# A list scheduler's time model in a one-core attention and mixer kernel: holding and seeing as two figures, block means on GpSimd, one weight sum later

## The chip, the cores and the metric

The kernel runs on one core of a Trainium2 chip. The core has five engines that run their own instruction streams and wait for one another by semaphores: TensorE (PE in the profile, its weight loads PEld), VectorE (DVE), ScalarE (ACT), GpSimd (POOL) and SyncE (SP), which here only issues DMA transfers. The metric is the device time of one execution in microseconds. A profiled execution gives, for each instruction, its engine, start and length, from which the views quoted below are made.

## The reference

Four batches of attention with eight heads of width 64 over 768 positions, each followed by a mixer with two pairs of matrices. All of it is float32.

```python
def _attn_ref(q, k, v):
    block, window = (32, 16)
    k_sum = k.reshape(B, H, nb, block, D).max(axis=3)
    v_sum = v.reshape(B, H, nb, block, D).mean(axis=3)
    scores_l = scale * np.matmul(q, k.transpose(0, 1, 3, 2))
    mask_l = np.abs(pos[:, None] - pos[None, :]) < window
    scores_s = scale * np.einsum('bhsd,bhnd->bhsn', q, k_sum) + np.log(block)
    scores_l_m = np.where(mask_l, scores_l, -1000000000.0)
    a = softmax(np.concatenate([scores_l_m, scores_s], axis=-1))
    return np.matmul(a, np.concatenate([v, v_sum], axis=2))

def _moe_ref(x, w_tok1, w_tok2, w_ch1, w_ch2):
    xt = x.transpose(0, 2, 1)
    h = np.maximum(xt @ w_tok1, 0.0) @ w_tok2
    u = x + h.transpose(0, 2, 1)
    h2 = np.maximum(u @ w_ch1, 0.0) @ w_ch2
    return u + h2
```

A position sees the keys less than 16 away from it and 24 block keys, each the maximum of 32 keys; the values of the block keys are the means of 32 values. The token matrices are 768 x 256 and 256 x 768, the channel matrices 512 x 1536 and 1536 x 512.

## The kernel before

**Attention.** Heads go in pairs, four pairs a batch; `p` counts the pairs over all batches, `g` is the half of the 768 positions. For a pair and a half, `scores` (products on PE, L467, line 467 of the kernel) multiplies queries with 96 window keys and 24 block keys. Then DVE adds the mask and takes each row's minimum (L481), and ACT takes the exponential and its row sums (L491). `turn` transposes the result on PE (L529) and copies it out with ACT (L540). In the last two batches the transposes go by DVE and DRAM instead. `weighted` multiplies with the values (L599) and scales the result with the reciprocal sums (L605 on POOL, L625 and L610 on DVE). `key_blocks` makes the block keys on DVE (L335, L344). For batch 0 alone `first_means` makes the block values: PE sums the values into two halves (L361), ACT copies one half (L372), DVE adds the other half, and the result, 24 rows for each head, is spread over twelve places of the value tile. For a pair's first head DVE adds once (`once`, L382) and POOL copies to all places (`spread`, L387); for its second head DVE adds straight into all places (`both`, L375).

**Mixer.** `tok1` (L753, L800, L837) and `tok2` (L912, L920) apply the token matrices, `ch1` (L981) and `ch2` (L1024) the channel matrices; float32 products are made from a high and a low part of each operand, three products each. Batches 0 to 2 run the channel matrices in slots: 12 slots of 512 columns and 12 of 256, in each of which stand one `ch1`, one `ch2` and a share of the next batch's attention. Batch 3, `last_batch` (L1251), uses sums and differences of weight blocks. These are made ahead by `mixes` (L1095 to L1152): POOL adds high and low parts and combines blocks, ACT and POOL split the result, and it is stored to DRAM. The table `MIXES` says in which slot each starts.

**Weights.** They arrive as 64-bit words and are decoded by `w_tick`, 30 ticks of two loads each: ACT takes an absolute value (`absolute`, L1665), POOL limits it (`clamp`, L1669), DVE does three steps (`shift` L1674, `sign` L1681, `low` L1688); from tick 3 on ACT and POOL split the result in high and low parts (L1712, L1718). Ticks 0 to 2 hold the first token matrix, 3 to 5 the second, and from 6 on two ticks belong to each of the twelve blocks of the channel matrices. All tick loads use buffers in which attention's tiles stood or will stand.

**Order.** The program does not emit instructions at once. `add` notes each piece of work with its engine, a duration in microseconds, what it reads and writes, a rank, and works that it may not start before (`behind`). `Plan._order` then simulates the engines: at each moment every free engine takes its ready work of the lowest rank, and of those the oldest. The order of the starts found so is the order in which the instructions are emitted; on the chip each engine keeps it and waits by semaphores. So a duration in `add` changes no instruction, but can change each engine's order. The ranks are `R_H, R_EVAC, R_ATT, R_LATER, R_W = range(5)` and `R_MIX = 6`; loads and stores have rank 0. The weight steps of ticks below `TOKT` have `R_ATT`, the later ones `R_W`.

In the simulation a work holds its engine for its duration; a DMA of `kb` thousand bytes starts when the earlier ones are through, at `RATE` per microsecond, and is seen `LAND` later. A work on another engine may start `LATE[engine]` after the end:

```python
late = self.LATE[e] if n.eng != e else 0.0
at = w.end + late if whole else now
```

Of the kernel before, what the change touches and what calls it, by code (L numbers as in the profile page):

```python
# [14 lines left out]
AF = mybir.ActivationFunctionType  # L15
# [63 lines left out]
class Plan:  # L79
    LATE = {"pe": 0.3, "act": 0.15, "dve": 0.15, "pool": 0.2, "sp": 0.0}  # L80
    RATE, LAND = 250.0, 2.2
# [46 lines left out]
    def _order(self):  # L128
# [9 lines left out]
        idle = {e: 0.0 for e in self.LATE}  # L138
        queues = {e: [] for e in self.LATE}
# [5 lines left out]
        for w in self.works:  # L145
            if not left[w]:
                release(w)
        while events:
# [5 lines left out]
            for e, queue in queues.items():  # L154
# [45 lines left out]
def tile_attention_mixer(  # L200
# [89 lines left out]
    def load(slot, view, src, kb, reads=(), behind=()):  # L290
        return add(
            "sp", 0.06, lambda: nc.sync.dma_start(out=view(slot.t), in_=src),
# [13 lines left out]
    def load_v(n):  # L306
# [7 lines left out]
        state["v"] = load(slot, lambda t: t[:WIN], vw[b, h], 295)  # L314
        if b > 0:
            s = vs[b]
            add(
                "sp", 0.06,
# [9 lines left out]
    def key_blocks(p):  # L328

        if p >= B * NP:  # L330
# [3 lines left out]
            "dve", 0.98,  # L334
# [8 lines left out]
            "dve", 0.33,  # L343
# [7 lines left out]
    def first_means(p):  # L351
# [22 lines left out]
        def both(n):  # L374
            nc.vector.tensor_tensor(  # L375
                out=v_t[n].t[WIN:NC],
                in0=half(1, 1).unsqueeze(1).broadcast_to([NB, NT, D]),
                in1=s.t[WIN:NC, D:].unsqueeze(1).broadcast_to([NB, NT, D]), op=ALU.add,
            )

        def once():
            nc.vector.tensor_tensor(  # L382
                out=s.t[WIN:NC, :D], in0=half(0, 1), in1=s.t[WIN:NC, :D], op=ALU.add
            )

        def spread(n):
            nc.gpsimd.tensor_copy(  # L387
                v_t[n].t[WIN:NC], s.t[WIN:NC, :D].unsqueeze(1).broadcast_to([NB, NT, D])
# [3 lines left out]
            "pe", 0.9, sums, reads=[(v_t[2 * p], 0), (v_t[2 * p + 1], 0)], writes=[(pt, 0)],  # L392
            rank=R_H,
        )
        for j in range(2):
# [3 lines left out]
        add("dve", 0.2, once, reads=[(pt, 0)], writes=[(s, 0)], rank=R_EVAC)  # L399
        add(  # L400
            "pool", 0.95, lambda: spread(2 * p), reads=[(s, 0)], writes=[(v_t[2 * p], 1)],
            rank=R_ATT,
        )
        add(
            "dve", 0.95, lambda: both(2 * p + 1), reads=[(pt, 0), (s, 1)],
            writes=[(v_t[2 * p + 1], 1)], rank=R_EVAC,
# [1490 lines left out]
```

## Time and profile before

| | |
|---|---|
| median of 3 runs | 560.07 us (559.93 to 560.61) |
| profiled execution | 559.61 us |
| its span, first to last instruction | 557.8 us |
| instructions | 12595 |
| TensorE's granted clock, mean | 1.000 |
| DMA, mean | 181 GB/s, 101.10 MB |

The profiled execution is one of its own, so sums over its rows are made against 559.61 us. The span ends 1.8 us below it. The profile's views that are read below: the busy time of each engine over the whole span, the same for stretches of the span, the waits of an engine (for which instruction, how long in all, how often, and the longest), groups of instructions by line with minimum, median and maximum of their lengths, and instructions in order of time, where several alike in a row are merged (`x24`) and the time in brackets is the engine's idle time just before and who ended it. The columns of a stretch are: from and to, length, busy time of PE, PEld, DVE, ACT and POOL with their counts, TensorE's clock, the DMA engines' busy share, and GB/s.

### The profile page before, as it was taken

The numbers are of one execution on the slowest core, as the hardware profiler recorded it, in microseconds if no ns is written. First come the engines' busy times: TensorE is split into PE (matmuls) and PEld (weight loads), VectorE is DVE, ScalarE is ACT, GpSimd is POOL, SyncE is SP. The second block draws the span as 40 slices with busy tenths as digits, with TensorE's granted clock in tenths as the row PEclk, the third lists the DMA queues.
The fourth block names the chain that finished last, engine by engine and source line by source line (L and its number), as shares of the span: only waits on it lengthen the run. The fifth ranks groups of instructions, "written<-read, shape, count | busy, mean of one in ns | idle before, by whom it ended". The sixth has DMA issues, their size and how long they took to land.

```text
span 557.8 us, 12595 instructions
## 1 busy us (share of the span) xinstructions
PE 544.0 (98%) x4557; PEld 479.6 (86%) x4557; DVE 330.3 (59%) x922; ACT 251.9 (45%) x784; POOL 246.8 (44%) x362
## 2 busy tenths in 40 slices
PE   7699999999999999999999999999999999999997
PEld 4588788888999978888799988878889999999997
DVE  4788999979365355454543247454352065669992
ACT  4786666625585344332323325343433453356410
POOL 0326687835574932310067404378769963000000
PEclk9999999999999999999999999999999999999999
DMA  8963668755668138768595316787696543932742
GB/s 277 330 189 108 215 209 249 240 163 190 203 187 251 42 131 226 198 207 226 146 253 137 104 29 196 160 237 198 171 259 168 135 155 116 333 95 81 219 134 85
DMA packets 125743, 101.10 MB, mean 181 GB/s; under 512 B 70000, under 2 KB 105456, under 8 KB 125680
## 3 DMA queue, kind: packets, MB, share of 16 engines
q1 hardware_dynamic: 125680, 100.29, 60.7%
q8 instruction: 36, 0.59, 0.5%
q14 instruction: 27, 0.22, 0.1%
HBM read 70.18 MB, written 28.31 MB: 177 GB/s over the span
## 4 chain that ended last, share of the span: by engine, by line
PE 90%; ACT 4%; DVE 3%; POOL 2%; issue 1%; ACTq 0%
PE acc L1024 27%; PE hp L981 27%; PE sc L467 4%; PE av L599 4%; PE up L920 3%; PE t1q L837 3%; ACT e L491 2%; PE x L1251 2%; PE y L1251 2%; PE z L1251 2%; PE pz L1251 2%; PE t1q L800 2%; PE up L1213 2%; PE warm L1731 1%; PE pw L1251 1%; PE pv L1251 1%
## 5 line engine op out<-in xcount | busy, mean ns | idle before, releaser
L1024 PE MATMUL acc<-h,w2h 128*128 128x256 f32 (+1 forms) x576 | 153.8, 339 | 0.0
L981 PE MATMUL hp<-u,w1h 128*128 128x256 f32 (+1 forms) x576 | 143.8, 339 | 0.0
L1024 PEld LDWEIGHTS acc<-h,w2h 128*128 128x128 f32 x576 | 100.6, 188 | 13.8 <-ACT h L993 1.6
L981 PEld LDWEIGHTS hp<-u,w1h 128*128 128x128 f32 x576 | 98.0, 189 | 12.4 <-issue 1.1
L981 PE MATMUL hp<-u,w1l 128*128 128x256 f32 (+1 forms) x288 | 96.9, 336 | 0.0
L491 ACT ACTIVATE e<-e,den 128x120 f32<-128x120 f32 x192 | 73.3, 384 | 52.0 <-DVE den L481 39.1
L1024 PE MATMUL acc<-h,w2l 128*128 128x256 f32 (+1 forms) x288 | 96.4, 335 | 0.0
L998 DVE SCALAR_TENSOR_TENSOR h<-hp,h 128x512 fp32r<-128x512 f32 (+1 forms) x72 | 39.9, 554 | 90.9 <-ACT h L993 90.7
L993 ACT ACTIVATE h<-hp 128x512 fp32r<-128x512 f32 (+1 forms) x72 | 35.2, 489 | 114.7 <-PE hp L981 114.5
L981 PEld LDWEIGHTS hp<-u,w1l 128*128 128x128 f32 x288 | 54.4, 189 | 5.8
L1024 PEld LDWEIGHTS acc<-h,w2l 128*128 128x128 f32 x288 | 54.2, 188 | 5.2
L481 DVE CUSTOM_DVE_ANT_0 e<-sc,mask_sb 128x120 f32<-128x120 f32 x192 | 41.7, 277 | 16.8 <-PE sc L467 16.2
L605 POOL TENSOR_SCALAR rec<-den 128x6 f32<-128x6 f32 x32 | 8.6, 269 | 66.1 <-ACT e L491 64.0
L491 ACT ACTIVATION_READ_ACCUMULATOR e<-e,den 128x1 f32 x192 | 36.1, 188 | 0.0
L1064 POOL TENSOR_TENSOR ot<-ot,u 128x512 f32<-128x512 f32 (+1 forms) x24 | 24.4, 1042 | 19.7 <-DVE ot L1056 18.2
L467 PE MATMUL sc<-k,q 64*64 64x120 f32 x768 | 28.0, 271 | 3.7 <-DVE den L481 2.2
L467 PEld LDWEIGHTS sc<-k,q 64*64 64x64 f32 x768 | 20.5, 132 | 12.5 <-issue 6.2
L920 PE MATMUL up<-wt2h,t 128*128 128x512 f32 (+1 forms) x96 | 28.4, 354 | 0.6 <-DVE t L739 0.6
L599 PEld LDWEIGHTS av<-v,eT 120*64 120x64 f32 x768 | 24.0, 138 | 4.7 <-issue 2.8
L599 PE MATMUL av<-v,eT 120*64 120x64 f32 x768 | 26.5, 224 | 0.9 <-PE hp L981 0.4
L335 DVE TENSOR_REDUCE ks<-k 128x24 f32<-128x768 f32 x16 | 15.2, 948 | 20.5 <-DMA k<-in_kw 20.5
L423 DVE TENSOR_REDUCE vs<-vb 96x8 f32<-96x256 f32 (+1 forms) x40 | 17.8, 458 | 9.4 <-DMA vb<-in_vb 9.3
(248 smaller groups left out, 1042.7 us busy)
## 6 DMA issues: line engine op xcount, KB each, us to landing
w<-in_w_ch SPq DMA_DIRECT2D x48, 256.0 KB
k<-in_kw SPq DMA_DIRECT2D x16, 720.0 KB
v<-in_vw SPq DMA_DIRECT2D x32, 288.0 KB
q<-in_q SPq DMA_DIRECT2D x16, 384.0 KB
away<-e SPq DMA_DIRECT2D x16, 384.0 KB
eT<-away SPq DMA_DIRECT2D x64, 96.0 KB
w<-in_w_tok SPq DMA_DIRECT2D x12, 256.0 KB
vb<-in_vb SPq DMA_DIRECT2D x32, 96.0 KB
```

The lines of the kernel that those rows point to most:

```text
L423: lambda: nc.vector.tensor_reduce(out=s.t[:VB, rows], in_=slot.t[:VB], axis=AX, op=ALU.add),
L467: nc.tensor.matmul(tiles[j].t[c * QT : (c + 1) * QT, i * NC : (i + 1) * NC], lhsT=qt.t[rows, t * QT : (t + 1) * QT], rhs=kt.t[rows, t, :], ...
L481: nc.vector.tensor_tensor_reduce(out=e.t[:, j, i * P : i * P + NC], in0=tiles[j].t[:, i * NC : (i + 1) * NC], in1=mask_sb[:, mv, :], op0=A ...
L491: nc.scalar.activation(ei, ei, AF.Exp, bias=den_t[n].t[:, 1, T : T + 1], scale=-1.0, accum_out=den_t[n].t[:, 0, T : T + 1],)
L599: nc.tensor.matmul(pv[cs, T], lhsT=eT[:NC, T % (TT // 2), cs], rhs=v.t[:NC, 2 * T + c], start=True, stop=True,)
L920: nc.tensor.matmul(pt.t[:, :nt], lhsT=t1.t[:, part, ks], rhs=w.t[:, k, h0 : h0 + nt], start=(far and k == 0 and i == 0), stop=(k == DTOK / ...
L981: nc.tensor.matmul(pt.t[:, :nt], lhsT=block(w, f, c), rhs=us[c].t[:, part], start=(i == 0), stop=(i == len(ops) - 1),)
L993: lambda: nc.scalar.activation(h.t[:, 0], pt.t[:, :nt], AF.Relu),
L998: lambda: nc.vector.scalar_tensor_tensor(out=h.t[:, 1], in0=pt.t[:, :nt], scalar=0.0, in1=h.t[:, 0].bitcast(F32), op0=ALU.max, op1=ALU.sub ...
L1024: nc.tensor.matmul(slot.t[:, c0 : c0 + nt], lhsT=block(w, f, o), rhs=h.t[:, part], start=(f == 0 and w == "w2h" and part == 0 and o % n == 0),
L1064: lambda view=view, u=u: nc.gpsimd.tensor_tensor(out=view(), in0=view(), in1=u.t[:, 1].bitcast(F32), op=ALU.add),
L1251: nc.tensor.matmul(pt.t[:, :cols], lhsT=w[wp][0](), rhs=z.t[:, zp], start=first and seen == 0, stop=final and seen == 3 * len(ops) - 1, sk ...
```

## The change

The planner gets two figures for each work in place of one: how long it holds its engine (`took`) and when its result is seen (`took` and `DRAIN` of its engine, and `NOTICE` of the engine that waits). Engines begin at `FIRST` and not at 0; a work that must only start behind another is seen `SEEN` later; a DMA begins `BEGIN` after its issue, at a higher `RATE` and with a shorter `LAND`. Some 60 durations are set anew; a DMA issue is now 0.44 on SP where most had 0.06, and some `kb` are raised. `first_means` loses `both`: for each head DVE adds once and POOL spreads, and both heads' copies have rank `R_ATT`. `TOKT` goes from 3 to 7. The weight sum `('w2', 4)` of batch 2 goes from slot 14 to slot 21, and such late sums are put behind their slot's `ch1`.

```diff
 class Plan:
-    LATE = {"pe": 0.3, "act": 0.15, "dve": 0.15, "pool": 0.2, "sp": 0.0}
-    RATE, LAND = 250.0, 2.2
+    FIRST = {"pe": 1.17, "act": 1.9, "dve": 0.85, "pool": 1.2, "sp": 0.7}
+    DRAIN = {"pe": 0.16, "act": 0.1, "dve": 0.08, "pool": 0.045, "sp": 0.0}
+    NOTICE = {"pe": 0.035, "act": 0.035, "dve": 0.035, "pool": 0.09, "sp": 0.035}
+    SEEN, BEGIN, LAND, RATE = 0.06, 1.34, 1.0, 375.0
...
-        idle = {e: 0.0 for e in self.LATE}
+        idle = dict(self.FIRST)
...
+        for e, at in idle.items():
+            heapq.heappush(events, (at, -1, None))
...
-                    dma = max(dma, now) + w.kb / self.RATE
+                    dma = max(dma, now + self.BEGIN) + w.kb / self.RATE
                     w.end = dma + self.LAND
                 else:
-                    w.end = now + w.took
+                    w.end = now + w.took + self.DRAIN[e]
...
-                    late = self.LATE[e] if n.eng != e else 0.0
-                    at = w.end + late if whole else now
+                    if not whole:
+                        at = now + self.SEEN
+                    elif n.eng != e:
+                        at = w.end + self.NOTICE[n.eng]
+                    else:
+                        at = idle[e] if e == "pe" else w.end
...
-        def both(n):
+        def once(j):
+            cs = slice(j * D, (j + 1) * D)
             nc.vector.tensor_tensor(
-                out=v_t[n].t[WIN:NC],
-                in0=half(1, 1).unsqueeze(1).broadcast_to([NB, NT, D]),
-                in1=s.t[WIN:NC, D:].unsqueeze(1).broadcast_to([NB, NT, D]), op=ALU.add,
-            )
...
+                out=s.t[WIN:NC, cs], in0=half(j, 1), in1=s.t[WIN:NC, cs], op=ALU.add
+            )
...
+        def spread(j):
             nc.gpsimd.tensor_copy(
-                v_t[n].t[WIN:NC], s.t[WIN:NC, :D].unsqueeze(1).broadcast_to([NB, NT, D])
-            )
...
+                v_t[2 * p + j].t[WIN:NC],
+                s.t[WIN:NC, j * D : (j + 1) * D].unsqueeze(1).broadcast_to([NB, NT, D]),
+            )
...
-        add("dve", 0.2, once, reads=[(pt, 0)], writes=[(s, 0)], rank=R_EVAC)
...
+        for j in range(2):
+            add(
+                "dve", 0.2, lambda j=j: once(j), reads=[(pt, 0)], writes=[(s, j)], rank=R_EVAC
+            )
+            add(
+                "pool", 0.95, lambda j=j: spread(j), reads=[(s, j)],
+                writes=[(v_t[2 * p + j], 1)], rank=R_ATT,
+            )
...
         add(
-            "pe", 0.95, products, reads=[(qt, 0), (kt, 0), (kt, 1)],
+            "pe", 0.776, products, reads=[(qt, 0), (kt, 0), (kt, 1)],
             writes=[(t, 0) for t in tiles], rank=R_H, behind=behind,
...
             add(
-                "pe", 0.5, flip, reads=[(e, (j, i)) for i in range(TT // 2)], writes=[(pt, 0)],
+                "pe", 0.33, flip, reads=[(e, (j, i)) for i in range(TT // 2)], writes=[(pt, 0)],
...
-    def mixes(k, i, tag, half=None):
+    def mixes(k, i, tag, half=None, behind=()):
...
-    TOKT = 3
+    TOKT = 7
...
-        stt = 0.7 if room else 0.85
+        stt = 0.6 if room else 0.75
...
-        add("dve", 0.69, shift, reads=parts, writes=[bkey], rank=rank)
+        add("dve", 0.596, shift, reads=parts, writes=[bkey], rank=rank)
...
-    add("pe", 7.0, warm_up, reads=[(warm, 0)], writes=[(pw, 0)])
+    add("pe", 4.6, warm_up, reads=[(warm, 0)], writes=[(pw, 0)])
...
-    MIXES = {..., (2, 14): [('w2', 4, 'h')], ...}
+    MIXES = {..., (2, 21): [('w2', 4, 'h')], ...}
...
-                mixes(*job)
+                mixes(*job, behind=here if slot > 14 else ())
```

More of the change, by code (lines that the diff above doesn't have):

```diff
@@ L137, in _order @@
         ready = {w: 0.0 for w in self.works}
-        idle = {e: 0.0 for e in self.LATE}
-        queues = {e: [] for e in self.LATE}
+        idle = dict(self.FIRST)
+        queues = {e: [] for e in idle}
         events, done, dma = [], [], 0.0
@@ L291, in load @@
         return add(
-            "sp", 0.06, lambda: nc.sync.dma_start(out=view(slot.t), in_=src),
+            "sp", 0.44, lambda: nc.sync.dma_start(out=view(slot.t), in_=src),
             reads=reads, writes=[(slot, 0)], kb=kb, behind=[*behind, *state["gate"]],
@@ L620, in weighted @@
             add(
-                "pool", 0.15, whole, reads=[(den, ("sum", T)) for T in range(TT)],
+                "pool", 0.166, whole, reads=[(den, ("sum", T)) for T in range(TT)],
                 writes=[(rec, 0)], rank=R_H,
@@ L628, in weighted @@
             add(
-                "dve", 0.57, scaled, reads=[(pt, 0), (rec, 0)], writes=[(x2, (hp % 2, j))],
+                "dve", 0.465, scaled, reads=[(pt, 0), (rec, 0)], writes=[(x2, (hp % 2, j))],
                 rank=R_EVAC,
@@ L737, in split_t1 @@
         add(
-            "dve", took + 0.05,
+            "dve", took + 0.065,
             lambda: nc.vector.scalar_tensor_tensor(
@@ L759, in tok1 @@
         add(
-            "pe", 2.8, products, reads=x_keys(b, p) + [(wt1, i) for i in range(3)],
+            "pe", 2.68, products, reads=x_keys(b, p) + [(wt1, i) for i in range(3)],
             writes=[(pt, 0)], rank=R_ATT,
@@ L808, in tok1x @@
             add(
-                "pe", 1.45, products, reads=[(s, i) for s in parts for i in range(2)],
+                "pe", 1.44, products, reads=[(s, i) for s in parts for i in range(2)],
                 writes=[(pt, 0)], rank=R_ATT,
@@ L843, in tok1_all @@
             add(
-                "pe", 1.37, products, reads=[(s, i) for s in (xs, ws) for i in range(2)],
+                "pe", 1.376, products, reads=[(s, i) for s in (xs, ws) for i in range(2)],
                 writes=[(pt, 0) for pt in pts], rank=R_ATT,
@@ L926, in tok2 @@
         add(
-            "pe", spent(nt, 0.75, 1.45) if far else spent(nt, 1.1, 2.0), products,
+            "pe", spent(nt, 0.707, 1.4) if far else spent(nt, 0.93, 1.837), products,
             reads=([] if far else x_keys(b, p)) + t1_keys(b, p) + T2_KEYS,
@@ L946, in tok2 @@
             )
-            eng, took = (("dve", spent(nt, 0.42, 0.62)), ("pool", spent(nt, 0.7, 1.2)))[half]
+            eng, took = (("dve", spent(nt, 0.34, 0.623)), ("pool", spent(nt, 0.7, 1.25)))[half]
             add(
@@ L1034, in ch2 @@
                 add(
-                    "pe", 3 * n * nt / 2220, lambda i=i: products(range(n * i, n * i + n)),
+                    "pe", 3 * n * nt / 2190, lambda i=i: products(range(n * i, n * i + n)),
                     reads=reads, writes=[(slot, 0)], rank=R_W,
@@ L1039, in ch2 @@
             add(
-                "pe", 12 * nt / 2220, lambda: products(range(NC4)), reads=reads,
+                "pe", 12 * nt / 2170, lambda: products(range(NC4)), reads=reads,
                 writes=[(slot, 0) for slot in slots], rank=R_W,
@@ L1098, in mixes @@
             add(
-                "pool", n * 0.0043 + 0.19, lambda x=x, f=f: whole(x, f),
-                reads=weight_keys(names, f), writes=[(a, x)], rank=R_MIX,
+                "pool", n * 0.0043 + 0.145, lambda x=x, f=f: whole(x, f),
+                reads=weight_keys(names, f), writes=[(a, x)], rank=R_MIX, behind=behind,
             )
@@ L1219, in tok2_last @@
         add(
-            "pe", 1.08, products, reads=t1_keys(b, p) + T2_KEYS, writes=[(pt, 0)], rank=R_ATT
+            "pe", 1.05, products, reads=t1_keys(b, p) + T2_KEYS, writes=[(pt, 0)], rank=R_ATT
         )
         add(
-            "dve", 0.56,
+            "dve", 0.474,
             lambda: nc.vector.tensor_tensor(
@@ L1259, in product @@
         return add(
-            "pe", 3 * len(ops) * cols / 2190, run, reads=list(reads), writes=[(pt, 0)], rank=R_W
+            "pe", 3 * len(ops) * cols / 2215, run, reads=list(reads), writes=[(pt, 0)], rank=R_W
         )
@@ L1736, in tile_attention_mixer @@
     add(
-        "sp", 0.06, lambda: nc.sync.dma_start(out=mask_sb, in_=mask), writes=[("mask", 0)], kb=184
+        "sp", 0.44, lambda: nc.sync.dma_start(out=mask_sb, in_=mask), writes=[("mask", 0)], kb=184
     )
```

135 lines of the change are left out of this document (62 added, 73 removed).

## The prediction

> **What bounds the kernel now.** I read the page's first part, then stretches of the span side by side, then TensorE's waits before 64 us. In the page:
> ```profile
> PE 544.0 (98%) x4557; PEld 479.6 (86%) x4557; DVE 330.3 (59%) x922; ACT 251.9 (45%) x784; POOL 246.8 (44%) x362
> ```
> TensorE (PE) is busy 544.0 of 557.8 us, so a change that leaves every matmul in place can win back at most the 13.8 us between. The view by stretches says where they lie (PE, then PEld, DVE, ACT, POOL; each busy time is followed by its count):
> ```profile
> 0.00:8.00 8.00, 6.83 (x45) 2.98 (x49) 1.92 (x5) 1.28 (x1) 0.76 (x7) 1.00 0.75 270
> 8.00:20.00 12.00, 8.61 (x230) 6.53 (x222) 8.98 (x53) 10.57 (x50) 1.30 (x3) 1.00 1.04 326
> 20.00:32.00 12.00, 7.85 (x119) 6.25 (x109) 10.49 (x36) 7.35 (x25) 4.18 (x6) 1.00 1.00 295
> 32.00:44.00 12.00, 12.00 (x288) 10.93 (x284) 10.59 (x43) 10.75 (x41) 5.14 (x9) 1.00 0.52 149
> 44.00:56.00 12.00, 11.70 (x116) 10.06 (x116) 9.53 (x28) 8.02 (x27) 7.80 (x11) 1.00 0.34 107
> 56.00:64.00 8.00, 7.17 (x54) 6.21 (x54) 7.22 (x14) 5.66 (x15) 5.13 (x8) 1.00 0.70 221
> 64.00:554.00 490.00, 489.60 (x3746) 436.64 (x3744) 281.03 (x750) 208.30 (x628) 222.50 (x321) 1.00 0.60 176
> 554.00:558.00 4.00, 0.27 (x2) 0.00 (x0) 0.56 (x1) 0.00 (x0) 0.00 (x0) 0.92 0.13 49
> ```
> From 64 to 554 us PE idles 0.40 us, at clock 1.00. The last 3.7 us are the last sum and its store, which the change leaves alone. The rest is at the front: 3.39 us from 8 to 20, 4.15 from 20 to 32, 1.13 from 44 to 64. There another engine is full: ACT 10.57 of 12 us in the first, DVE 10.49 of 12 in the second. The DMA share is full from 8 to 32 us as well, but no DMA stands among PE's waits up to 64 us:
> ```profile
> PE t1p L753 <- DVE wt L1688: 2.3, 2, 1.3
> PE sc L467 <- DVE den L481: 2.2, 2, 1.6
> PE sc L467 <- ACT eT L540: 1.6, 2, 1.3
> PE et L529 <- ACT e L491: 1.3, 3, 0.7
> ```
> In these four, which are most of it, DVE is named for 4.5 us and ACT for 2.9. So the kernel is a filled PE behind a 64 us front, and the change is worth what it does to the front, plus what order costs inside PE's full stretch.
>
> **The spread of the means.** For each of batch 0's four pairs `both` on DVE (L375) goes. One more small sum (L382) and one more copy on POOL (L387) come:
> ```profile
> L375 DVE TENSOR_TENSOR v<-vm,vs x4: 965/965/965, 15.9 to 42.8; 24x768 f32<-24x768 f32 x4
> L382 DVE TENSOR_TENSOR vs<-vm,vs x4: 220/220/222, 15.6 to 42.5; 24x64 f32<-24x64 f32 x4
> L387 POOL COPY v<-vs x4: 822/824/827, 16.0 to 43.0; 24x768 f32<-24x768 f32 x4
> ```
> DVE is relieved of 0.965 - 0.220 = 0.745 us a pair, 2.98 us in all; POOL, which is busy 24.30 of the first 64 us, gets 4 x 0.824 = 3.3 us. Not all four count. The second pair's stands in front of a wait of PE:
> ```profile
> 21.13 0.96 DVE L375 TENSOR_TENSOR v<-vm,vs 24x768 f32<-24x768 f32 x1
> 22.43 0.28 DVE L481 CUSTOM_DVE_ANT_0 e<-sc,mask_sb 128x120 f32<-128x120 f32 x1
> 22.77 1.04 PE L467 MATMUL sc<-k,q 64*64 64x120 f32 x24 [1.63 <-DVE den L481]
> ```
> DVE runs without a gap here and PE waits 1.63 us for the minimum at its end, so this wait shrinks by **0.74 us** (bounds 0 and 0.74). The three decodes after it, which two more waits name, move up with it; that is the same gain, not another. The first pair's wins nothing, for ACT is full there; the third and fourth (36 and 43 us) fall where PE idles nothing. They come due later, in two waits behind a DVE that is by then busy with weights:
> ```profile
> 60.71 0.73 PE L920 MATMUL up<-wt2h,t 128*128 128x512 f32 x2 [0.61 <-DVE t L739]
> 62.13 0.44 PE L912 MATMUL up<-identf,x 128*128 128x128 f32 x2 [0.22 <-DVE u L964]
> ```
> With 1.49 us less ahead of it on DVE I take both as gone: **0.83 us** (bounds 0 and 0.83). The second head's values now wait for two copies in a row on POOL, 1.65 us after the sum, where `both` needed 0.96: 0.7 us later. PE has the first head's half of these products to do meanwhile, 0.81 us:
> ```profile
> 31.69 1.62 PE L599 MATMUL av<-v,eT 120*64 120x64 f32 x48
> ```
> POOL's `rec` and `clamp` queue behind the second copy, and DVE's `shift` waits for `clamp`; without that cover it costs up to 0.7 us once.
>
> **The planner's two figures and its costs.** They add and remove no instruction: what can differ is each engine's order and that of the DMA issues on SP. In the front a better order can win no more than the fullest engine has to spare: 12 - 10.57 = 1.43 us on ACT up to 20 us and 12 - 10.49 = 1.51 on DVE up to 32, together 2.94. A worse one can lose as much. I take a third, **1.0 us**. Some of the old costs are far off and others fit, as two steps of a weight's decode show:
> ```profile
> L1674 DVE TENSOR_SCALAR wt<-wt x3: 416/427/427, 23.1 to 27.8; 128x512 int32<-128x512 int32 x3
> L1681 DVE SCALAR_TENSOR_TENSOR wt<-w,wt x3: 691/693/693, 23.6 to 28.2; 128x512 int32<-128x512 int32 x3
> ```
> `shift` was planned at 0.69 us and takes 0.427, `sign` at 0.7 and takes 0.693. So the old order is by partly wrong times, but two engines that are each seven eighths full leave little to sort.
>
> In the full stretch an order costs PE where the kind of matmul changes:
> ```profile
> 118.61 0.78 PE sc L467 x24
> 119.39 2.95 PE acc L1024 x12
> 122.34 2.72 PE hp L981 x12
> ...
> 408.24 2.95 PE acc L1024 x12
> ```
> Behind scores a group of twelve takes 2.95 us, behind its like 2.72: 0.23 a change. The chain of work has 23 such groups of 512 columns, the first and the last of them shown, 5.3 us. The pieces that cause them stay, and they only lie together or apart: **0**, with five changes either way as bounds, 1.2 us.
>
> **Ticks 3 to 6 at the attention's rank (TOKT).** No work is added. A tick is 0.427 + 2 x 0.693 = 1.81 us on DVE (`low`, L1688, takes what `sign` does, below), now taken by age rather than when nothing else is ready. Cover is the stretch from 32 to 44 us, where PE has 12.00 of 12 us of ready work. I cost it at 0; one tick in front of a set of scores with no cover is 1.8 us.
>
> **The weight sum that moves.** Its 2 + 4 + 2 POOL instructions, 2 of ACT and its 2 stores on SP go from slot 14 to 21, gated by slot 21's first product. But the old one starts late already, behind the store that frees its buffers:
> ```profile
> 445.47 1.45 PE hp L981 x12
> ...
> 448.49 2.54 POOL L1095 TENSOR_TENSOR wa_w_None<-w2h,w2l 128x512 f32<-128x512 f32 x2 [2.35 <-DMA mix_w2h<-wa_w_None]
> ```
> 445.47 is the tenth of half 1's twelve, slot 21: the gate opens before the old start. **0**; POOL idles from 480 us on, so even 5 us more is covered.
>
> **Sum.** 0.74 + 0.83 + 1.0 = 2.57 us off the profiled run's 559.61 us is 557.0; that run stands 0.46 below the median of 560.07, so against the median I forecast **557.5**.
>
> **Rivals.** (a) *The weights take over as the bound.* An earlier PE meets the decode:
> ```profile
> 64.00:118.00 54.00, 54.00 (x241) 44.72 (x240) 51.28 (x93) 32.23 (x79) 41.27 (x61) 1.00 0.71 224
> 69.42 1.46 POOL L1718 TENSOR_TENSOR w1l<-wb,w1h 128x256 fp32r<-128x256 f32 x2 [0.59 <-ACT w1h L1712]
> 72.21 0.62 PE L981 MATMUL hp<-u,w1h 128*128 128x512 f32 x2
> ```
> DVE is 95% busy, and the third weight is ready 72.21 - 70.88 = 1.33 us before its use. If the chain of decodes does not move up with PE, 1.33 us is all: 558.7. Against it: DVE's 2.98 us lie ahead of this chain.
>
> (b) *POOL's copies take back what they relieve.* A decode's last step beside a POOL instruction took 0.979 us instead of 0.693:
> ```profile
> L1688 DVE SCALAR_TENSOR_TENSOR wt<-w,wt x3: 691/693/979, 24.3 to 29.0; 128x512 int32<-128x512 int32 x3
> 26.36 0.77 POOL L1669 TENSOR_SCALAR wt<-wt 128x512 f32<-128x512 f32 x1 [0.90 <-ACT wt L1665]
> 26.68 0.98 DVE L1688 SCALAR_TENSOR_TENSOR wt<-w,wt 128x512 int32<-128x512 int32 x1
> ```
> That is 0.29 us a meeting, up to a whole copy, 0.824, which is more than a pair's 0.745. The first two terms then go and the order's 1.0 stays: 559.1. The Trainium skill, "SBUF — State Buffer", section "Who interferes with whom", has such a rule: VectorE with two SBUF inputs and a GpSimd instruction that reads SBUF lock each other out for a whole instruction. By that rule the four new copies could cost 4 x 0.82 us; the row, 0.29 for 0.45 us of overlap, agrees in kind. For the copies no row shows it: `both`, which reads PSUM, kept 965 ns in all four, beside them.
>
> (c) *No effect.* ACT and DVE are as full as before in another order, and the relief falls into their own gaps: 560.0.
>
> (d) *Slower, by ticks 3 to 5.* Their words are loaded here, and these minima are the third pair's:
> ```profile
> 21.79 6.74 SPq L1635 DMA_DIRECT2D w<-in_w_tok  x5
> 31.75 0.24 DVE L481 CUSTOM_DVE_ANT_0 e<-sc,mask_sb 128x120 f32<-128x120 f32 x1
> ```
> Words that land before 31.75 us put up to 3 x 1.81 = 5.4 us of decoding in front of the minima. From the point where PE's ready work is shorter than that, it starves; with half uncovered it loses 2.7 us: 562.8. For it: the second pair's wait has just this form, DVE work ahead of minima. Against it: PE's full 12 us there.
>
> **How the numbers follow.** Forecast 0.52, (a) 0.13, (b) 0.06, (c) 0.12, (d) 0.17. The forecast's own ends are 560.07 - 0.74 - 0.83 - 2.94 - 1.2 = 554.4 and, with nothing won in the front and 1.2 lost to changes, 561.3; the range of 554.6 to 561.2 leaves out most of (d) and the tips. A measurement of this kernel tells about 0.2%, 1.1 us, from no change. Faster by more: 0.51 of the forecast, 0.09 of (a), 0.02 of (b), 0.62; within: 0.01, 0.04, 0.04 and (c)'s 0.12, 0.21; slower: (d), 0.17.
>
> **What would show it.** Right: PE's first `hp` starts near 61.5 us and not at 64.0, the wait of 1.63 us is below 1, the two at 60 us are gone, and from there to the end the length is what it was within 1.2 us. (a) shows as new waits of `hp` or `acc` for L1718; (b) as L1681 or L1688 over 0.9 us beside L387; (d) as waits of `sc` or `et` behind L1674 to L1688 from 31 to 44 us. The forecast is wrong if PE's idle time before 64 us stays near 9.85 us, or if the stretch behind it grows.

## The result, and the profile after

The changed kernel takes 591.04 us (median of six, 588.10 to 594.21), the kernel before beside it 560.50 us (median of six): a ratio of 1.0543, with a 95% interval of 1.0505 to 1.0582. It is 5.4% slower, where 557.5 us was forecast. The profiled execution, the slowest of the six, took 594.21 us with a span of 592.4 us, 34.6 us more than before.

The page's first, second and fourth parts for the changed kernel: busy time by engine, the granted clock in 40 slices of the span, and the chain of work that ended last.

```profile
PE 559.7 (94%) x4557; PEld 490.5 (83%) x4557; DVE 322.4 (54%) x922; ACT 252.5 (43%) x784; POOL 251.0 (42%) x366
...
PEclk9999999989999999899997999999999999999999
...
PE 65%; DMA 11%; DVE 9%; ACT 4%; POOL 4%; SPq 3%; issue 3%; POOLq 0%; ACTq 0%; DVEq 0%
```

The chain of the kernel before, for comparison:

```profile
PE 90%; ACT 4%; DVE 3%; POOL 2%; issue 1%; ACTq 0%
```

The matmuls are the same 4557. Yet PE idles 592.4 - 559.7 = 32.7 us instead of 13.8, and is busy 559.7 us instead of 544.0. So 18.9 us of the loss are waits, and 15.7 us are the same matmuls taking longer, most of it at the places where the clock row falls. Of the chain 11% now goes to DMA, which had no share of it before, and 9% to DVE. The view by stretches says where (columns as before the prediction: PE, PEld, DVE, ACT and POOL with counts, TensorE's clock, DMA share, GB/s):

```profile
0.00:64.00 64.00, 54.45 (x795) 42.10 (x796) 45.86 (x172) 42.75 (x155) 29.99 (x46) 0.97 0.70 224
64.00:118.00 54.00, 54.00 (x248) 44.95 (x247) 49.21 (x94) 33.03 (x80) 41.17 (x61) 1.00 0.65 198
118.00:470.00 352.00, 332.34 (x2798) 285.88 (x2797) 151.12 (x527) 131.41 (x460) 162.05 (x240) 0.97 0.60 167
470.00:554.00 84.00, 84.00 (x524) 82.98 (x523) 53.02 (x96) 39.35 (x82) 17.75 (x20) 1.00 0.44 143
```

The same stretch of the kernel before:

```profile
118.00:470.00 352.00, 351.60 (x3024) 307.99 (x3023) 167.04 (x561) 141.79 (x488) 181.23 (x261) 1.00 0.61 172
```

From 118 to 470 us PE was full; now it idles 19.66 us there and its clock averages 0.97. PE's waits in that stretch (total, times, longest) name the cause:

```profile
PE av L601 <- DMA eT<-away: 9.5, 4, 2.9
PE av L601 <- issue: 4.9, 3, 3.4
PE sc L469 <- DVE den L483: 3.0, 1, 3.0
PE sc L469 <- DMA q<-in_q: 2.1, 1, 2.1
```

These four make 19.5 of the 19.66 us, and the kernel before idles 0.40 us there in all. For 11.6 us the profile names a transfer. The 3.0 us for DVE's minima go back to one as well: these minima stand in DVE's stream behind a reduction of the keys, which starts at 127.24 us, when `k` has landed, and PE goes on at 129.94.

```profile
127.24 0.95 DVE L343 TENSOR_REDUCE ks<-k 128x24 f32<-128x768 f32 x1 [6.51 <-DMA k<-in_kw]
```

For the 4.9 us under "issue" the profile names no releaser, so what these products wait for is open. In the new order, then, PE comes to `av` and to `sc` before their data have landed. Behind them in PE's stream stand `hp` and `acc` matmuls, and PE takes its stream in order.

**One such wait.** `turn` stores to DRAM (`away<-e`) and loads back transposed (`eT<-away`); `weighted` (`av`) needs the loads. Here are SP's issues and PE's products for one set, from the changed kernel's order in time (start, length, instruction; in brackets PE's idle time before it):

```profile
226.34 0.34 SPq L558 DMA_DIRECT2D away<-e  x1
228.80 2.77 SPq L576 DMA_DIRECT2D eT<-away  x4
...
232.36 2.66 SPq L576 DMA_DIRECT2D eT<-away  x4
...
235.53 0.57 PE L601 MATMUL av<-v,eT 120*64 120x64 f32 x12
238.05 1.52 PE L601 MATMUL av<-v,eT 120*64 120x64 f32 x36 [1.95 <-DMA eT<-away]
```

The first four loads bring one half of the positions, the second four the other. The first twelve products need the first half alone. They start 235.53 - 232.36 = 3.17 us after the first of the second four loads is issued, and the other 36 have to wait until 238.05, 5.69 us after it. In the kernel before, the first products of this kind stood 5.93 us behind the second four, and did not wait:

```profile
217.91 2.66 SPq L574 DMA_DIRECT2D eT<-away  x4
...
223.84 1.62 PE L599 MATMUL av<-v,eT 120*64 120x64 f32 x48
```

All eight sets of such loads show the same: in the kernel before, the first product stands 4.8 us or more behind the second four. In the changed kernel it is 2.1 to 3.2 us in the four sets that wait for `eT`, and 5.5 or more in the others.

The old planner reckoned each of these loads as 150/250 = 0.6 us and saw it 2.2 us later; the new one reckons 150/375 = 0.4 us, not before 1.34 us after the issue, and sees it 1.0 later. For a load by itself these come to nearly the same, 2.8 and 2.7 us. For four that find earlier transfers under way it is 4 x 0.6 + 2.2 = 4.6 us against 4 x 0.4 + 1.0 = 2.6, where the wait above ended after 5.69. So the new plan lets `av` come sooner than the transfers do.

**The clock behind the wait.** The record of the granted clock in this trace changes only on a fixed grid of 3.41 us. Three steps of that grid around the wait above, in the view by stretches:

```profile
235.52:238.94 3.42, 1.47 (x43) 1.32 (x44) 1.63 (x4) 0.90 (x2) 1.31 (x2) 0.99 0.76 201
238.94:242.35 3.41, 3.41 (x21) 2.72 (x17) 2.51 (x5) 0.00 (x0) 0.14 (x1) 0.50 0.54 138
242.35:245.76 3.41, 3.41 (x21) 2.89 (x20) 0.42 (x1) 0.38 (x1) 0.00 (x0) 1.00 0.93 277
```

PE is busy 1.47 of 3.42 us in the first step, and the next step, with PE full, runs at 0.50. So a wait of 1.95 us is paid once as idle time and again as half of 3.41 us, 1.7 us. The record has seven such steps, behind six waits between 118 and 470 us, 23.9 us at half clock, and one in the front, 3.4 us. Half of 23.9 is 11.9 us. That and the 19.7 us of waits are 31.6 us. The first `hp` is 2.43 us later than before:

```profile
66.45 0.63 PE L983 MATMUL hp<-u,w1h 128*128 128x512 f32 x2
```

Together 34.0 of the 34.6 us: the change lost little in the front, where it was to win, and nearly all of it in the stretch that was full. Up to its first `hp` PE idles 9.55 us, and 9.85 before, so the front's loss is longer matmuls, 1.7 us of it by the step at half clock.

### The profile page after: what moved, and what is told of

Its sections match the earlier page's. It is cut to its first block, busy times and chain, and to the rows that moved or that the text cites. A ratio compares the mean times of both kernels' runs of the same rounds, so it can differ in the third digit from the quotient of the medians.

```text
span 592.4 us, 12619 instructions
## 1 busy us (share of the span) xinstructions
PE 559.7 (94%) x4557; PEld 490.5 (83%) x4557; DVE 322.4 (54%) x922; ACT 252.5 (43%) x784; POOL 251.0 (42%) x366
## 4 chain that ended last, share of the span: by engine, by line
PE 65%; DMA 11%; DVE 9%; ACT 4%; POOL 4%; SPq 3%; issue 3%; POOLq 0%; ACTq 0%; DVEq 0%
PE acc L1026 18%; PE hp L983 16%; DMA k<-in_kw 3%; PE up L922 3%; PE av L601 3%; PE sc L469 3%; PE t1q L839 3%; SPq L576 3%; DMA w<-in_w_ch 2%; DMA eT<-away 2%; PE x L1253 2%; PE y L1253 2%; PE z L1253 2%; PE pz L1253 2%; ACT e L493 2%
## 5 line engine op out<-in xcount | busy, mean ns | idle before, releaser
L1026 PE MATMUL acc<-h,w2h 128*128 128x256 f32 (+1 forms) x576 | 158.5, 347 | 0.0
L983 PE MATMUL hp<-u,w1h 128*128 128x256 f32 (+1 forms) x576 | 145.3, 342 | 0.0
L1026 PEld LDWEIGHTS acc<-h,w2h 128*128 128x128 f32 x576 | 103.8, 194 | 14.5 <-ACT h L995 1.6
L983 PEld LDWEIGHTS hp<-u,w1h 128*128 128x128 f32 x576 | 99.7, 192 | 12.4 <-issue 1.1
L1026 PE MATMUL acc<-h,w2l 128*128 128x256 f32 (+1 forms) x288 | 98.4, 342 | 0.0
L1026 PEld LDWEIGHTS acc<-h,w2l 128*128 128x128 f32 x288 | 55.9, 194 | 5.3
L601 PE MATMUL av<-v,eT 120*64 120x64 f32 x768 | 30.3, 236 | 15.3 <-DMA eT<-away 9.5
L601 PEld LDWEIGHTS av<-v,eT 120*64 120x64 f32 x768 | 27.0, 148 | 20.1 <-issue 16.6
L469 PE MATMUL sc<-k,q 64*64 64x120 f32 x768 | 29.7, 281 | 6.7 <-DVE den L483 4.1
L469 PEld LDWEIGHTS sc<-k,q 64*64 64x64 f32 x768 | 21.9, 138 | 16.2 <-issue 12.9
L343 DVE TENSOR_REDUCE ks<-k 128x24 f32<-128x768 f32 x16 | 15.2, 948 | 27.8 <-DMA k<-in_kw 27.8
```

The costliest lines, as they stand in the source:

```text
L469: nc.tensor.matmul(tiles[j].t[c * QT : (c + 1) * QT, i * NC : (i + 1) * NC], lhsT=qt.t[rows, t * QT : (t + 1) * QT], rhs=kt.t[rows, t, :], ...
L601: nc.tensor.matmul(pv[cs, T], lhsT=eT[:NC, T % (TT // 2), cs], rhs=v.t[:NC, 2 * T + c], start=True, stop=True,)
L983: nc.tensor.matmul(pt.t[:, :nt], lhsT=block(w, f, c), rhs=us[c].t[:, part], start=(i == 0), stop=(i == len(ops) - 1),)
L1026: nc.tensor.matmul(slot.t[:, c0 : c0 + nt], lhsT=block(w, f, o), rhs=h.t[:, part], start=(f == 0 and w == "w2h" and part == 0 and o % n == 0),
```

## The experiments

Theories at the start: **the DMA figures** (`RATE`, `LAND`, `BEGIN` and the raised `kb`) bring PE too early to data that go through DRAM; against it, **the structure** (spread means, `TOKT`, the later sum), **the two figures** (`FIRST`, `DRAIN`, `NOTICE`, `SEEN`), or **the durations**. Here are all kernels, with the span of each profiled execution split into PE's idle and busy time (the page's span less PE's busy time, and that time), and the time at half clock up to 540 us from the record of the clock.

| kernel | median us | ratio to before, 95% | PE idle | PE busy | at half clock |
|---|---|---|---|---|---|
| before | 560.5 | | 13.8 | 544.0 | 0 |
| after | 591.04 | 1.0543 (1.0505 to 1.0582) | 32.7 | 559.7 | 27.3 |
| e2_planner | 591.54 | 1.0554 (1.0505 to 1.0603) | 35.5 | 553.8 | 17.1 |
| e4_dma_new | 580.31 | 1.0354 (1.0258 to 1.0449) | 23.0 | 553.5 | 10.2 |
| e3_dma_old | 573.18 | 1.0227 (1.0165 to 1.0288) | 20.8 | 551.6 | 17.1 |
| e5_turn_slow | 572.36 | 1.0208 (1.0168 to 1.0248) | 20.3 | 550.0 | 6.8 |
| e12_durations | 571.87 | 1.0197 (1.0172 to 1.0221) | 17.9 | 552.3 | 17.1 |
| e13_two_figures | 571.35 | 1.0187 (1.0163 to 1.0212) | 16.3 | 553.3 | 17.1 |
| e6_best | 567.49 | 1.0123 (1.0064 to 1.0181) | 14.8 | 549.3 | 10.2 |
| e16_late_less | 567.34 | 1.0114 (1.0081 to 1.0147) | 17.4 | 549.4 | 10.2 |
| e7_spread | 566.80 | 1.0109 (1.0078 to 1.0139) | 15.2 | 549.5 | 13.7 |
| e15_late_more | 565.86 | 1.0087 (1.0066 to 1.0109) | 13.6 | 550.4 | 13.7 |
| e10_wait_long | 565.75 | 1.0080 (1.0019 to 1.0140) | 16.2 | 545.9 | 3.4 |
| e1_structure | 563.99 | 1.0073 (1.0037 to 1.0110) | 14.2 | 548.4 | 10.2 |
| e14_wait_mid | 562.84 | 1.0044 (1.0029 to 1.0059) | 12.4 | 547.7 | 6.8 |
| e8_tokt | 562.74 | 1.0053 (1.0029 to 1.0078) | 14.3 | 546.8 | 6.8 |
| e11_same_order | 561.16 | 1.0015 (1.0001 to 1.0029) | 12.4 | 549.3 | 13.7 |
| e9_wait_short | 561.00 | 1.0023 (0.9994 to 1.0052) | 13.1 | 545.9 | 6.8 |
| e17_filler | 560.28 | 0.9987 (0.9969 to 1.0005) | 10.6 | 546.9 | 3.4 |

Each ratio is against runs of the kernel before on the same chip, whose medians were 560.40 to 561.30 us. The medians of e2 to e5, e12, e13, e15 and e16 are of two runs each, the others of 3 to 10.

### The parts: structure or planner, and which figure of it

**e1_structure** keeps the old planner and all durations but one and makes the three other parts of the change (the spread as in its diff, and these two); **e2_planner** is the changed kernel without these three.

```diff
-    TOKT = 3
+    TOKT = 7
...
-    MIXES = {..., (2, 14): [('w2', 4, 'h')], ...}
+    MIXES = {..., (2, 21): [('w2', 4, 'h')], ...}
```

> The kernel before with its old planner and all its old durations, and only the three parts of the change that alter the program: means spread by POOL, TOKT 7, the weight sum in slot 21. If the loss comes from the planner's figures, this lies near before, between 556 and 563 us, with a granted clock of 1.00. If it comes from these three parts (the ticks ahead of attention, or the sum in slot 21), it is slower by most of 30 us, 580 or more.

> The changed kernel without the three parts: the new planner's figures and durations alone. If the figures cause the loss: 580 to 595 us, with waits of PE for DMA behind 118 us and a clock below 0.99. If the three parts cause it: 556 to 563 us.

Measured 563.99 and 591.54 us. The planner alone makes the whole loss; what the three parts cost on the old planner, 3.5 us, does not show on the new one. The structure theory falls for the large loss.

**e3_dma_old** is the changed kernel with the DMA figures of before, **e4_dma_new** the kernel before with the new ones. e3's edit, which e4's turns round:

```diff
-    SEEN, BEGIN, LAND, RATE = 0.06, 1.34, 1.0, 375.0
+    SEEN, BEGIN, LAND, RATE = 0.06, 0.0, 2.2, 250.0
...
-        state["v"] = load(slot, lambda t: t[:WIN], vw[b, h], 413)
+        state["v"] = load(slot, lambda t: t[:WIN], vw[b, h], 295)
...
-                writes=[keys[j]], kb=375, behind=behind,
+                writes=[keys[j]], kb=262, behind=behind,
```

> The changed kernel with only the DMA figures of before in its planner (250 per us, seen 2.2 us later, no delay at the start, the old sizes of the value and weight loads). Theory DMA (the planner believes that transfers land sooner than they do, and PE, which keeps the planned order, stands before data that is not there): the waits of av for eT<-away and of sc for q go, and the time falls to 556 to 566 us. Theory durations (the other new figures pack the engines too tightly): it stays above 580 us.

> The kernel before with only the new DMA figures in its planner. Theory DMA: it gets most of the loss, 575 to 595 us, and waits of PE for DMA show up between 118 and 470 us. Theory durations: it stays within 3 us of before, 557 to 564 us.

The new DMA figures alone put 20 us on the kernel before (580.31), and the old ones take 18 us off the changed kernel (573.18). The long stretch of e3, and e4's largest wait:

```profile
118.00:470.00 352.00, 349.98 (x2989) 303.35 (x2988) 165.83 (x558) 141.65 (x489) 180.96 (x262) 1.00 0.62 174
```

```profile
PE av L599 <- DMA eT<-away: 7.7, 5, 3.1
```

So the waits for `eT` come with the DMA figures and go with them. Most of what e3 still loses lies in its front: PE is busy 49.35 of the first 64 us, and 54.15 before.

**e5_turn_slow** is the changed kernel, with one thing said otherwise to the planner: the transfers of `turn` and of the tokens through DRAM, and the block values' copies, count for half as much again. Three of the five edits:

```diff
-            reads=[(e, part) for part in PARTS], writes=[(away, 0)], kb=393,
+            reads=[(e, part) for part in PARTS], writes=[(away, 0)], kb=590,
...
-            lambda t: flat(t).rearrange("p (t q c) -> p t q c", q=P // 32, c=32), 150,
+            lambda t: flat(t).rearrange("p (t q c) -> p t q c", q=P // 32, c=32), 225,
...
-            from_sources, nt // 8, behind,
+            from_sources, nt * 3 // 16, behind,
```

> The changed kernel, its planner told only that the transfers of attention through DRAM (away, eT, xaway, xT) and of the value means are half as large again, which gives them back the speed that they were planned with before. If these transfers make the waits of the full stretch: the waits of av for eT<-away go and the time is 570 to 576 us, as with all the old DMA figures. If the old 2.2 us of landing or the k and q loads are what is missed: 580 us or more.

It takes 572.36 us: five sizes win back 18.7 of the 31 us, with no instruction changed. The largest three of PE's waits of e5 between 118 and 470 us, and the stretch:

```profile
PE av L601 <- issue: 2.9, 2, 2.2
PE sc L469 <- DVE den L483: 1.6, 1, 1.6
PE t1q L802 <- POOL ws L788: 0.8, 1, 0.8
```

```profile
118.00:470.00 352.00, 345.25 (x2951) 299.56 (x2951) 159.80 (x549) 140.14 (x484) 175.16 (x254) 1.00 0.62 173
```

No wait for `eT` is left, and the idle time of the stretch falls from 19.66 to 6.75 us. That the sizes were too small for these transfers is shown. Why e5 still waits for `av` with "issue", where the profile names no releaser, is open.

**e12_durations** gives the kernel before only the new durations (the lines of the change's diff such as 0.95 to 0.776), **e13_two_figures** only the new handling of holding and seeing, with the DMA figures of before in both. e13's figures, whose use is that of the change's diff:

> The kernel before with all the new durations of its works (SP's 0.44 among them), but the old way of counting ends and the old DMA figures. If the new durations order the front badly or let the clock fall there: 565 to 575 us with a full stretch behind 64 us. If they are harmless: 559 to 562 us.

```diff
-    LATE = {"pe": 0.3, "act": 0.15, "dve": 0.15, "pool": 0.2, "sp": 0.0}
-    RATE, LAND = 250.0, 2.2
+    FIRST = {"pe": 1.17, "act": 1.9, "dve": 0.85, "pool": 1.2, "sp": 0.7}
+    DRAIN = {"pe": 0.16, "act": 0.1, "dve": 0.08, "pool": 0.045, "sp": 0.0}
+    NOTICE = {"pe": 0.035, "act": 0.035, "dve": 0.035, "pool": 0.09, "sp": 0.035}
+    SEEN, BEGIN, LAND, RATE = 0.06, 0.0, 2.2, 250.0
```

> The kernel before with only the two figures (when engines begin, the drain of each, the notice of the one that waits), old durations and old DMA figures. If these make a part of the loss: 564 us or more. If not: 558 to 562 us.

Each alone costs 11 us, which the DMA figures do not explain. With the DMA figures' 20 that makes 42, where the planner as a whole costs 31 (e2): the parts do not add up, since each leads to another order. The first 64 us of e12, in which PE idles 12.5 us and runs at a mean clock of 0.87:

```profile
0.00:64.00 64.00, 51.48 (x746) 39.99 (x747) 42.71 (x159) 38.09 (x142) 18.41 (x35) 0.87 0.61 197
```

e13 loses in both places: its first `hp` starts at 69.17 us, 5.15 later than before, and in the full stretch one wait of 3.6 us is followed by two steps at half clock. PE waits for POOL's split of `xs`, which stands in POOL's stream behind a weight sum that waits for a store:

```profile
PE t1q L845 <- POOL xs L889: 3.6, 1, 3.6
...
455.62 1.26 POOL L1103 TENSOR_TENSOR wa_w_None<-w2h,w2l 128x512 f32<-128x512 f32 x1 [6.59 <-DMA mix_w2h<-wa_w_None]
```

So an order can stall the full stretch with the old DMA figures too, and the engine that stands for a transfer need not be PE.

**e6_best** puts the new DMA figures and e5's sizes into the kernel before.

> The kernel before with the new DMA figures in its planner, and the same transfers planned half as large again. If only these transfers are planned too fast: the stretch behind 64 us is as full as before, the front keeps the 3 us less of PE idle time that it has with the new DMA figures, and the time is 556 to 560 us. If the figures are wrong in other places too: 565 to 580 us.

567.49 us: 13 us better than e4, and 7 us slower than before. In its long stretch PE idles 2.5 us, 0.8 of them for `eT`, and its front waits 5.4 us for the values' loads. So the five sizes were the largest error of the DMA figures, and not the only one.

### The parts of the structure

**e7_spread** makes only the spread of the means on the kernel before, as the change's diff of `first_means` has it (with it one duration of PE there falls from 0.9 to 0.8, in e1 too), **e8_tokt** only this:

> The kernel before with the means spread by POOL and nothing else. If DVE's relief stands on PE's path: 557 to 559.5 us. If the reordered front idles long enough that the granted clock falls, it carries the loss of the three parts: 562 to 566 us.

```diff
-    TOKT = 3
+    TOKT = 7
```

> The kernel before with TOKT 7 and nothing else. If ticks 3 to 6 displace attention in the front: 562 to 566 us, with waits of PE before 64 us that are longer than before's 9.85 us. If not: 559.5 to 561 us, and the loss of the three parts is the spread's or the late sum's.

The spread, from which the forecast had 1.57 us of gain, costs 6.3 us with the order that it leads to; `TOKT` costs 2.3. Both lose up to 67 us; behind it, and up to 554 us, PE is full at clock 1.00. Steps of the clock's grid in e7's front:

```profile
8.60:12.01 3.41, 1.96 (x34) 1.12 (x22) 3.31 (x23) 3.01 (x16) 0.00 (x0) 1.00 1.06 278
12.01:15.43 3.42, 3.13 (x73) 2.67 (x73) 1.77 (x18) 3.23 (x16) 0.47 (x2) 0.50 1.03 318
15.43:18.84 3.41, 3.41 (x67) 2.89 (x66) 0.54 (x4) 2.77 (x12) 1.59 (x2) 0.50 1.03 382
```

PE is busy 1.96 of 3.41 us, and the two next steps run at half clock. The kernel before is no fuller there, and kept its clock in the profiled execution:

```profile
14.63:18.04 3.41, 2.10 (x51) 1.53 (x50) 1.80 (x9) 3.16 (x15) 0.82 (x1) 1.00 1.01 372
18.04:21.45 3.41, 2.75 (x86) 2.21 (x80) 2.66 (x9) 2.40 (x12) 0.29 (x1) 1.00 1.06 401
21.45:24.87 3.42, 1.84 (x30) 1.43 (x31) 3.14 (x9) 2.85 (x9) 2.54 (x5) 1.00 1.04 312
```

It does not always. Of 13 runs of it on one chip, three had a mean clock of 1.000 and took 558.62 to 559.04 us, three had 0.988 and took 561.55 to 562.36, and the others lay between. The front is full enough to hold the clock in some executions and not in others.

**e11_same_order** asks for the spread without another order: the second head's copy goes to POOL, with durations in the plan under which PE, ACT and SP keep their order, and DVE and POOL differ in four instructions each.

```diff
+                    if w.took == 0.0 and w.eng == "pool":
+                        at = now
...
-            "dve", 0.95, lambda: both(2 * p + 1), reads=[(pt, 0), (s, 1)],
-            writes=[(v_t[2 * p + 1], 1)], rank=R_EVAC,
+            "dve", 0.95, lambda: both(2 * p + 1), reads=[(pt, 0)],
+            writes=[(s, 1)], rank=R_EVAC,
+        )
+        add(
+            "pool", 0.0, lambda: spread1(2 * p + 1), reads=[(s, 1)],
+            writes=[(v_t[2 * p + 1], 1)], rank=R_H,
```

> The kernel before with the means spread by POOL, and its planner given such durations that every engine keeps the order of before: DVE's order differs in four instructions (a sum of 64 columns in place of 768), POOL's in four copies more, PE's, ACT's and SP's in none. If DVE's relief is worth what the prediction gave it when nothing else moves: 557.5 to 559.5 us. If POOL's copies cost as much as they relieve: 560 to 561 us. The spread alone with a new order took 566.8 us; if the moved work itself makes that, this is above 563 us.

561.16 us, ratio 1.0015 (1.0001 to 1.0029). PE's waits up to 64 us, first rows:

```profile
PE t1p L762 <- DVE wt L1697: 2.5, 2, 1.7
PE sc L476 <- DVE den L490: 1.7, 2, 1.1
```

The wait for the minima falls from 1.63 to 1.1 us, as forecast in kind, and the time does not fall with it. In the profiled execution, which was the slowest of the ten, four steps at half clock stood in the front. None of its runs kept a mean clock of 1.000. At a mean clock of 0.993 to 0.994, seven of its runs have a median of 561.06 us, and eleven of the kernel before beside them 560.65: at the same clock no gain is seen either. Whether the relief is worth anything at a full clock is not shown.

**e15_late_more** and **e16_late_less** change no kernel idea at all: `LATE` is 0.02 us longer or shorter for PE, ACT, DVE and POOL.

```diff
-    LATE = {"pe": 0.3, "act": 0.15, "dve": 0.15, "pool": 0.2, "sp": 0.0}
+    LATE = {"pe": 0.32, "act": 0.17, "dve": 0.17, "pool": 0.22, "sp": 0.0}
```

> The kernel before with the planner's delay between engines raised by 0.02 us on each engine (LATE 0.32, 0.17, 0.17, 0.22) and nothing else: a change without meaning that moves some works in the front. If the order of before is an ordinary one, this lies within 2 us of it, 558.5 to 562.5 us, and the new figures are worse than the old in the front. If the order of before is a lucky one among many like it, this loses as e7, e12 and e13 did: 563 to 572 us.

> The same with 0.02 us less on each engine. Ordinary order: 558.5 to 562.5 us. Lucky order: 563 to 572 us.

They cost 4.6 and 6.0 us against 561.30 beside them. A twitch of 20 ns in the model moves the order enough for 1%, both ways the same sign. Of these three orders that of before is the best, so a change to the plan can cost this much whatever it means. The structure's parts, 2.3 to 6.3 us, are of this size too. The 18 to 20 us of the DMA figures are not, and their waits name the transfers.

### What a wait of PE costs

Three kernels add to the kernel before one product in batch 1's slot 8 that the output doesn't use; it waits for a row of POOL memsets, 20, 31 or 36.

```diff
+            if b == 1 and slot == 8:
+                def hold():
+                    for _ in range(36):
+                        nc.gpsimd.memset(probe, 0.0)
...
+                add("pool", 0.1, hold, writes=[("probe", 0)], rank=R_H, behind=here)
```

> The kernel before with one extra matmul of PE in batch 1, slot 8, that waits for 20 small memsets of POOL which the planner holds for 0.1 us: a wait of PE of 1 to 1.5 us in its full stretch. If a wait costs its own length: 560.07 plus that, 561 to 562 us, clock 1.00. If every wait also lowers the clock: 562.5 us or more.

> The same with 36 memsets, a wait of PE of 4 to 5 us. If a wait costs its own length: 564 to 565 us at a clock of 1.00. If a wait of over about 2 us halves the clock for some 3 us behind it, as the changed kernel's trace shows six times: 566 to 567.5 us, with a stretch at 0.50 right behind the wait.

> The kernel before with one extra matmul that waits for 31 memsets of POOL: between the 20 that hid behind PE's work and the 36 that made it wait 2.5 us and lowered its clock, so a wait of about 1.5 us. If the clock falls only behind waits of about 2 us and more: 561.5 to 562.5 us with a clock of 1.00 in the full stretch. If it falls behind any wait: 563 to 564 us, 0.50 for some 3 us behind it.

All three waits came out shorter than planned. With 20 memsets PE did not wait, and the time is that of before within the interval. With 36 it waits 2.54 us; the row of the product, and the clock's grid:

```profile
259.07 0.49 PE L1829 MATMUL probe<-probe 128*128 128x128 f32 x2 [2.54 <-POOL probe L1823]
...
256.54:259.95 3.41, 0.88 (x5) 0.80 (x6) 0.58 (x2) 0.60 (x1) 2.43 (x12) 1.00 0.98 282
259.95:263.36 3.41, 3.41 (x10) 2.64 (x9) 2.67 (x6) 0.00 (x0) 0.00 (x0) 0.50 0.71 273
```

With 31 it waits 1.25 us:

```profile
258.69 0.49 PE L1829 MATMUL probe<-probe 128*128 128x128 f32 x2 [1.25 <-POOL probe L1823]
...
255.50:258.91 3.41, 2.16 (x11) 1.49 (x10) 0.34 (x4) 2.34 (x11) 2.65 (x13) 1.00 0.95 226
258.91:262.33 3.42, 3.42 (x17) 2.83 (x17) 2.00 (x5) 0.00 (x0) 0.29 (x2) 1.00 1.01 295
```

The long wait leaves PE busy 0.88 of 3.41 us, and the next step is at half clock; the middle one leaves 2.16, and the clock stays. The long one's span is 562.1 us, with no other step at half clock: 4.3 over before, which is 2.54 of wait and 1.71 of clock. So it is shown by a wait that was put there, and not only read from the changed kernel, that such a wait costs more than its own length. The medians, 5.3 and 2.4 us over before, hold the front's clock too, which differs from run to run.

**e17_filler** adds twelve products on zeros at the lowest rank after the first scores, to hold the front's clock; the output doesn't use them.

```diff
+        if s == 1:
+            scored = [w for w in plan.works if w.eng == "pe"][-1]
+            for _ in range(12):
+                add(
+                    "pe", 0.25,
+                    lambda: nc.tensor.matmul(
+                        pw.t, lhsT=warm.t[:, :P], rhs=warm.t, start=True, stop=True
+                    ),
+                    reads=[(warm, 0)], writes=[(pw, 0)], rank=R_MIX, behind=[scored],
+                )
```

> The kernel before with twelve matmuls more on zeros, which the planner may put where it sees PE idle behind the first scores. If the dips of the clock in the front cost before the 1 to 2 us by which its runs differ, and fillers hold the clock: 558.5 to 560 us. If the fillers stand in the way of work that PE waits for: 561 us or more.

560.28 us against 561.30, ratio 0.9987 (0.9969 to 1.0005): no gain is shown. Its runs had mean clocks of 0.993 to 1.000, and before's there 0.988 to 0.994, so the clock did rise; the fillers may also have changed the order. No kernel here is shown to beat the one before.

## Why the prediction was wrong

**The step that failed** is "In the full stretch an order costs PE where the kind of matmul changes", costed at 0 with 1.2 us as bounds. The stretch lost 31.6 us: 19.7 of waits and 11.9 of clock. The bound priced changes of kind, which may have kept to it, for only 0.6 of the 34.6 us is left beside these terms and the front's. It had nothing for a wait of PE, and no reason was given for that. The prediction took a PE without gaps there as a fact of the kernel. It was a fact of the order: the old plan kept `av` 4.8 us or more behind the second four of its loads, and with the new DMA figures alone (e4) the waits for `eT` appear. That the new figures were quicker stood in the diff, and the SP rows of the loads beside the products would have shown the distance that the old order kept.

**The rivals** lacked this one: the head of an engine's stream, PE's above all, standing for a transfer. The slower side, (d), had the sign by another mechanism. Its place, waits of `sc` or `et` behind ticks from 31 to 44 us, shows 1.2 us of `et` behind `x` (L612) and nothing behind a tick. (a) falls, for no `hp` or `acc` waits for L1720, and (c) by the size. (b)'s mechanism is there. These are decode steps on DVE and copies on POOL of the changed kernel, from its order in time:

```profile
37.12 1.20 DVE L1683 SCALAR_TENSOR_TENSOR wb<-w,wb 128x512 int32<-128x512 int32 x1
39.99 0.68 DVE L1683 SCALAR_TENSOR_TENSOR wb<-w,wb 128x512 int32<-128x512 int32 x1
46.66 1.20 DVE L1683 SCALAR_TENSOR_TENSOR wb<-w,wb 128x512 int32<-128x512 int32 x1
```

```profile
36.95 0.82 POOL L389 COPY v<-vs 24x768 f32<-24x768 f32 x1 [0.83 <-POOL wb L1671]
40.02 1.33 POOL L389 COPY v<-vs 24x768 f32<-24x768 f32 x1
46.23 1.08 POOL L389 COPY v<-vs 24x768 f32<-24x768 f32 x1
```

In these three pairs whichever starts second is longer by 0.5 us: the step at 37.12 and at 46.66 (1.20 for 0.69), the copy at 40.02 (1.33 for 0.82); the copy at 46.23 is longer too, 1.08. The rule of the Trainium skill that the prediction weighed, "SBUF — State Buffer", "Who interferes with whom", agrees in kind with these rows. But the price, 2 x 0.5 us on DVE, is no part of the 31 us, for PE does not wait for DVE's decoding where these are lost.

**What bounds the kernel** was read rightly as a limit on gains, 13.8 us. It is no limit on losses: PE's idle time can be any length, and the same matmuls can take longer.

**The spread, 0.74 + 0.83 us.** The second pair's wait did fall below 1, as forecast, and of the two waits at 60 us one is still there, so the 0.83 was not won. Two rows of PE's waits up to 64 us in the changed kernel:

```profile
PE sc L469 <- DVE den L483: 1.1, 2, 0.7
...
PE up L922 <- DVE t L741: 0.5, 1, 0.5
```

Neither reached the time: the first `hp` starts at 66.45 us, and not near 61.5. With the order held, e11, the gain is not there either.

**The planner's figures, 1.0 us within 2.94.** The sign was wrong; the front lost 2.43 us in the changed kernel, and 9.1 in e12, whose first `hp` starts at 73.11 us. PE's idle time before 64 us stayed at 9.55 us, near the 9.85 that the prediction named as a sign of being wrong. "A worse one can lose as much" had no row behind it: the spare of the fullest engine bounds a gain alone. A loss adds the steps at half clock, which the forecast's terms did not have. The clock of 1.00 in every row before the change was read as given, though windows with PE busy 1.84 of 3.42 us stood in that front.

**Ticks at the attention's rank, 0.** e8 shows 2.3 us on the old planner. At a mean clock of 1.000 it is 3.4 us (five runs with a median of 562.05 us, against three of before at 558.64), so the clock is not the whole of it. Among PE's waits in its front is a new one, for a split weight of such a tick, and two steps of the grid are at half clock:

```profile
PE av L599 <- POOL wt2l L1718: 2.3, 1, 2.3
```

The wait is near the 1.8 us that the prediction gave an uncovered tick, on POOL and not on DVE.

**The moved sum, 0.** It was not tried alone. With the other two parts it changes nothing that can be measured on the new planner (e2 beside after), and from 470 to 554 us PE is full as before. The sum that stalls e13 is this one at its old place; whether its move alone would have spared that was not tried.

**The range** was too narrow because its ends came from the front's terms and the changes of kind. Nothing in it stood for an order that is wrong about DMA, or for a loss of clock.

## What to carry to other kernels

In a list schedule that is fixed before the run, look first at landings that the plan reckons too early: the engine in order then stands still with other work behind it, and here 19.7 us of standing cost another 11.9 in clock. Calibrate transfers by their shape, from the distance between issue and use in a trace, not by one rate. Before you credit an edit to a plan, run the plan with its constants moved by a few hundredths: here that alone cost about 1%, more than any part of the structure was meant to win.

## What the runs showed of the hardware

In these traces the granted clock changes only on a fixed grid of 3.41 us, and it goes with what PE did in the step before. Over the profiled executions of all nineteen kernels, without the first 6 us and the last steps of each span, steps at full clock were followed by one at half clock in 20 of 20 cases with PE busy less than 44% of the step, in 20 of 28 between 44 and 56%, in 8 of 28 between 56 and 64%, and in none of more than 2900 above 64%. Between 44 and 64% the busy share alone does not decide. The Trainium skill, "TensorE: Matmul & The Clock Gate", Part 1, has the free-running window of 3413 ns and the half clock behind an idle window, and the traces agree. Its rule of no idle gaps beyond some 3.4 us is too mild here: 1.95 us of waiting was enough in the changed kernel, 2.54 in e10, and in e7's front a step with PE 57% busy was followed by half clock, though no wait there was longer than 0.69 us. A step at half clock with PE busy over 97% was followed by full clock in 42 of 42 cases; with PE busy less than 90%, in none of 11.
